# Putting DMA-transposed q and k in token order on ScalarE: planes read in a row and written at a stride of 6, instead of read at a stride and written in a row

## The chip, the cores and the metric

The kernel runs on one core of a Trainium2 chip. The metric is the device time of one execution in microseconds (us); smaller is better. Before the change the median of three runs was 346.24 us (345.09 to 347.84). Runs of one kernel scatter by about half a per cent (the eleven runs of the kernel before made beside experiment 11: 345.25 to 349.92 us, standard deviation 0.5%), so every comparison below uses runs made in turn on the same chip. A run counts as slow when it lies over 1.5% above the fastest run of the same kernel, and as fast otherwise; ratios use fast runs alone. The engines are called PE (TensorE, matmuls), ACT (ScalarE), DVE (VectorE), POOL (GpSimd) and SP (which issues DMAs).

## The reference, cut to what matters

```python
# q, k, v: 8 batches, 8 heads, 576 tokens, 64 channels, float32, 0.1 x normal
q_d, k_d, v_d = means of q, k, v over groups of 4 tokens
out_d     = softmax(q_d k_d^T / 8) v_d           # 144 x 144, then each row repeated 4 times
out_local = softmax of q k^T / 8 where |i - j| < 4, times v
x = (out_up + out_local), as 4608 tokens x 512
h = x @ w_in                                      # 512 x 2048
out = (h - tanh(h)) @ w_out                       # 2048 x 512, float32
```

Of the kernel before, what the change touches and what calls it, by code (L numbers as in the profile page):

```python
# [15 lines left out]
class Program:  # L16
# [18 lines left out]
    def op(self, eng, ns, fn, reads=(), writes=(), pri=0):  # L35
        i = len(self.ops)
        deps = set()
        for key in reads:
            if key in self.last_write:
                deps.add(self.last_write[key])  # L40
        for key in writes:
            if key in self.last_write:
                deps.add(self.last_write[key])
            deps.update(self.readers.get(key, ()))
        for key in reads:
            self.readers.setdefault(key, set()).add(i)
        for key in writes:
            self.last_write[key] = i
            self.readers[key] = set()
        deps.discard(i)  # L50
        self.ops.append((eng, ns, fn, deps, pri))
        self.touch.append(set(reads) | set(writes))
        return i
# [97 lines left out]
def kernel(  # L151
# [18 lines left out]
    A6 = 6  # L170
# [12 lines left out]
    def fixed(name, shape, dt, n=None, pool=const):  # L183
        if n is None:
            return pool.tile(shape, dt, name=name, tag=name)
        return [pool.tile(shape, dt, name=f"{name}{i}", tag=f"{name}{i}")
                for i in range(n)]
# [15 lines left out]
    qT = fixed("qT", [128, 2, A6, G6], BF16, 2)  # L203
# [198 lines left out]
    def attention(p):  # L402
        b, j, hb, s, jj = p // NP, p % NP, p // 2, p % 2, p % 2
# [9 lines left out]
        for i in range(2):  # L413
# [3 lines left out]
                      for eng, ns, fn in REORDER[p >= NEARLY][i]],  # L417
# [3 lines left out]
        full = bass.AP(tensor=qk[s].tensor, offset=qk[s].offset,  # L421
                       ap=[qk[s].ap[0], [KOFF, 2], [1, 576]])
        if p >= T_DMA:
            op("SP", 700, lambda: nc.sync.dma_start_transpose(
                out=qT[s].rearrange("p i a g -> p (i a) g"),
                in_=qr[s].rearrange("p i a c -> p (i a c)")),
               reads=[("qr", s, 0), ("qr", s, 1)],
               writes=[("qT", s), ("qTq", s)], pri=-50)
            op("DMA", 1300, None, reads=[("qTq", s), ("qr", s, 0), ("qr", s, 1)],
               writes=[("qT", s)], pri=pri)  # L430
            for i in range(2):
                op("ACT", 600, lambda i=i: A.copy(  # L432
                    out=full[:, i].rearrange("p (g a) -> p g a", a=A6),
                    in_=qT[s][:, i].rearrange("p a g -> p g a")),
                   reads=[("qT", s)], writes=[("qk", s, i)], pri=pri)
        else:
            for i in range(2):
                b16 = ps[:, i].bitcast(BF16)[:, 0:S]

                def tr(i=i, b16=b16):  # L440
                    for a in range(A6):
                        T.transpose(b16[:, G6 * a:G6 * a + G6], qr[s][:, i, a, :],  # L442
                                    ident[0:G6, 0:G6])
                if i == 0:
                    P.fresh.add(len(P.ops))
                op("PE", 260 * cold, tr, reads=[("qr", s, i), "ident"],
                   writes=[(t, i) for t in ts], pri=pri)
                op("ACT", 540, lambda i=i, b16=b16: A.copy(  # L448
                    out=full[:, i].rearrange("p (g a) -> p g a", a=A6),
                    in_=b16.rearrange("p (a g) -> p g a", a=A6)),  # L450
                   reads=[(t, i) for t in ts], writes=[("qk", s, i)], pri=pri)
# [54 lines left out]
        else:  # L506
# [5 lines left out]
            out=e1, in_=ps[:, :, 0:480], func=AF.Exp, scale=SCALE),  # L512
           reads=ts, writes=[("E", s, 0)], pri=pri)
        op("DVE", 700, lambda: V.tensor_tensor(  # L514
            out=e1, in0=e1,
# [3 lines left out]
        if not new:  # L519
            op("PE", 380 * cold, s2, reads=qks + [("qkd", s)], writes=ts, pri=pri)  # L520
        op("ACT", 240, lambda: A.activation(
            out=e2v, in_=ps2[:, :, 0:96], func=AF.Exp, scale=SCALE),
           reads=ts2, writes=[("E", s, 1)], pri=pri)
        op("ACT", 560, lambda: A.activation(
            out=e3, in_=ps2[:, :, 96:384], func=AF.Exp, scale=SCALE / 16.0),
           reads=ts2, writes=[("E", s, 2)], pri=pri)
        op("DVE", 220, lambda: V.tensor_tensor(
            out=e2v, in0=e2v,
# [5 lines left out]
        def outs():  # L534
# [22 lines left out]
            out=ln[s].rearrange("p n (h d) -> p h n d", d=D),  # L557
# [14 lines left out]
        if p >= X_DMA:  # L572
            op("SP", 600, lambda: nc.sync.dma_start_transpose(
                out=lT[s], in_=ln[s].rearrange("p n c -> p (n c)")),
# [25 lines left out]
            out=xT[j][:, b * S:(b + 1) * S].rearrange("p (g a) -> p g a", a=4),  # L600
# [106 lines left out]
    for i in range(NVW):  # L707
        def ones(i=i):
# [5 lines left out]
            out=vd[i][:, 1, :, 64], in_=vd[i][:, 1, :, 64], compare_op=ALU.is_ge,  # L714
# [46 lines left out]
    for i in range(2):  # L761
        op("DVE", 70, lambda i=i: V.memset(qkd[i][:, 288:344], 0.0),
           writes=[("qkd", i)], pri=-94)
        op("DVE", 70, lambda i=i: V.memset(vp[i][:, :, :, 64:65], 4.0),
           writes=[("vp", i)], pri=-94)
    work = [attention(p) for p in range(NPAIR)]
    for a in work:
        next(a)
# [65 lines left out]
```

## The kernel before: the parts that the change touches

Two heads are processed as a pair, 32 pairs in all. For a pair, q and k arrive with six neighbouring tokens per partition (96 partitions x 6 tokens). They are cast to bf16 and transposed, so that channels lie on partitions. The transposition yields six *planes*: plane `a` holds tokens a, 6+a, 12+a and so on. Someone must then put the planes in token order. Pairs 0 to 15 are transposed by PE into PSUM, and ACT reads the planes from there. Pairs 16 to 31 are transposed by DMA into SBUF (`qT`), and ACT puts them in order in `qk`; this is the code that changes.

```python
# qT[s]: [128, 2 (q, k), 6 planes, 96] bf16;  qk[s]: [128, 1192] bf16; q at element 0, k at 585
full = bass.AP(tensor=qk[s].tensor, offset=qk[s].offset, ap=[qk[s].ap[0], [KOFF, 2], [1, 576]])
if p >= T_DMA:                                   # T_DMA = 16
    op("SP", 700, ... nc.sync.dma_start_transpose(out=qT[s] ..., in_=qr[s] ...) ...)
    for i in range(2):
        op("ACT", 600, lambda i=i: A.copy(                                        # L432
            out=full[:, i].rearrange("p (g a) -> p g a", a=A6),
            in_=qT[s][:, i].rearrange("p a g -> p g a")),
           reads=[("qT", s)], writes=[("qk", s, i)], pri=pri)
else:
    ...                                          # PE transposes; the same A.copy out of PSUM: L448
# then: POOL adds neighbours of q and k (half L459, qkd L464); PE: scores L478 and L494;
# ACT: exp L511, L521, L524; DVE: mask of E L514, L527; PE: E times v L538, L545; ...
```

The dense part is woven in between. Per 512 tokens, it has 16 groups of 4 matmuls into a PSUM buffer (L619), a tanh by ACT (L627), a subtraction by DVE (L630), and the second matmuls (L646), whose results ACT copies out (L657). There are four such PSUM buffers.

The order of instructions on each engine is fixed when the program is built. A planner simulates the program with an assumed cost for each operation and emits it in the order that it finds. The assumed cost of the copy above is 600 ns. It is an input of the plan alone; it changes nothing that the instruction does.

```python
def op(self, eng, ns, fn, reads=(), writes=(), pri=0): ...     # ns: assumed cost
def order(self):  # per step: the engine that can start earliest takes its ready operation of least pri
```

The softmax here doesn't subtract the row's maximum and nothing guards it: scores larger than these inputs give would overflow.

## Time and profile before

| what | before |
|---|---|
| time, median of 3 | 346.24 us |
| PE busy | 328.0 us of 346.3 |
| ACT busy | 224.8 us |
| the 32 copies of L432 | 37.0 us, 1168 to 1225 ns each, 120.9 to 244.7 us |
| the copies out of PSUM (L448), same walk | 633 to 676 ns each (means of the groups 641 and 643) |

The page of the profile shows one execution. Its first row gives the busy time of each engine, with its share of the span; the rows of digits below it split the span in 40 slices and show the busy share of each in tenths.

```profile
span 346.3 us, 6847 instructions
PE 328.0 (95%) x2556; PEld 163.5 (47%) x2556; DVE 223.8 (65%) x362; ACT 224.8 (65%) x382; POOL 169.9 (49%) x210
...
PE   6787989999999999999999999899999999999995
ACT  4585886768978768787878778599753434343411
```

PE is the bound: it is busy nine tenths and more of nearly every slice. The copies, instruction by instruction (minimum, median, maximum in ns):

```profile
L432 ACT COPY qk_88<-qT_90 x16: 1168/1186/1216, 120.9 to 236.2; 128x576 bf16<-128x576 bf16 x16
L432 ACT COPY qk_89<-qT_91 x16: 1173/1188/1225, 129.6 to 243.5; 128x576 bf16<-128x576 bf16 x16
```

The table of stretches gives the busy time of each engine within the stage that has these copies.

```profile
core 0: us, PE busy (x) PEld busy (x) DVE busy (x) ACT busy (x) POOL busy (x), PEclk, DMA share, GB/s
120.00:270.00 150.00, 147.23 (x1139) 72.01 (x1138) 112.02 (x168) 110.98 (x173) 96.50 (x109) 1.00 0.86 179
```

PE works 147.2 of the 150 us. What it waits for in this stage is in the view of waits, for PE from 118 to 275 us (who waited, for whom, us in total, times, longest):

```profile
PE ps_ox L538 <- DVE E_100 L527: 1.5, 3, 0.7
PE ps_ox L538 <- DVE E_100 L514: 0.4, 2, 0.2
PE ps_ox L538 <- DVE E_101 L514: 0.4, 1, 0.4
```

That is 2.3 us. Summed by engine, the chain of work that ended last reads:

```profile
PE 69%; DVE 10%; ACT 9%; issue 3%; DMA 3%; POOL 2%; SPq 1%; ACTq 0%; POOLq 0%; DVEq 0%
```

### The profile page before, as it was taken

How to read it: one execution, taken by the hardware profiler on the slowest of the kernel's cores; microseconds unless marked ns; L12 is line 12 of the kernel's file. 1: busy time of each engine (PE TensorE's matmuls, PEld its weight loads, DVE VectorE, ACT ScalarE, POOL GpSimd, SP SyncE). 2: the span in 40 equal slices, each digit the busy share in tenths (PEclk: the TensorE clock that was granted, in tenths of full speed). 3: DMA queues.
4: the chain of work that ended last, by engine and by line, in shares of the span. 5: the costliest groups of instructions: out<-in, count | busy, mean ns of one | idle time of the engine just before them, and what ended most of it. 6: DMA issues, size and time to landing. Idle time of an engine off the chain costs nothing.

```text
span 346.3 us, 6847 instructions
## 1 busy us (share of the span) xinstructions
PE 328.0 (95%) x2556; PEld 163.5 (47%) x2556; DVE 223.8 (65%) x362; ACT 224.8 (65%) x382; POOL 169.9 (49%) x210
## 2 busy tenths in 40 slices
PE   6787989999999999999999999899999999999995
PEld 2353445555555554445444444444454444444442
DVE  5675788558897968778867677679774443343300
ACT  4585886768978768787878778599753434343411
POOL 6553555575467856887777786958500000000000
PEclk9698999999999999999999999999999999999999
DMA  8999999999999998999999999645231000100021
GB/s 192 234 374 300 277 262 263 217 216 287 212 222 234 252 234 174 226 231 235 261 221 207 260 233 246 157 92 93 57 85 60 31 32 30 61 32 31 30 93 61
DMA packets 103407, 60.74 MB, mean 175 GB/s; under 512 B 77774, under 2 KB 94670, under 8 KB 103374
## 3 DMA queue, kind: packets, MB, share of 16 engines
q1 hardware_dynamic: 103374, 60.30, 78.5%
q8 instruction: 20, 0.33, 0.4%
q14 instruction: 13, 0.11, 0.1%
HBM read 42.46 MB, written 9.44 MB: 150 GB/s over the span
## 4 chain that ended last, share of the span: by engine, by line
PE 69%; DVE 10%; ACT 9%; issue 3%; DMA 3%; POOL 2%; SPq 1%; ACTq 0%; POOLq 0%; DVEq 0%
PE ps_hy_540 L646 8%; PE ps_hy_538 L619 8%; PE ps_hy_539 L619 7%; PE ps_hy_541 L646 7%; PE ps_hy_538 L646 7%; PE ps_hy_539 L646 6%; PE ps_hy_540 L619 6%; PE ps_hy_541 L619 6%; PE ps_ox L538 3%; DVE qr_87 L416 2%; PE ps_ts L478 2%; DMA qkn_73<-in_k_dram 2%; PE ps_ox L545 2%; PE ps_ts L442 2%; PE ps_ox L389 2%
## 5 line engine op out<-in xcount | busy, mean ns | idle before, releaser
L619 PEld LDWEIGHTS <-w_in_sb 128*128 128x128 bf16 x576 | 53.3, 98 | 62.1 <-issue 3.9
L646 PEld LDWEIGHTS <-gT_110 128*128 128x128 bf16 x320 | 30.2, 98 | 34.5
L646 PEld LDWEIGHTS <-gT_111 128*128 128x128 bf16 x256 | 24.0, 98 | 27.4
L459 POOL TENSOR_TENSOR half<-qk_88 128x576 f32<-128x576 bf16 x14 | 16.4, 1169 | 25.3 <-ACT qk_88 L448 11.2
L459 POOL TENSOR_TENSOR half<-qk_89 128x576 f32<-128x576 bf16 x16 | 18.7, 1167 | 19.8 <-ACT qk_89 L448 12.2
L646 PE MATMUL ps_hy_539<-w_out_sb,gT_110 128*128 128x512 bf16 x80 | 20.7, 379 | 0.0
L646 PE MATMUL ps_hy_540<-w_out_sb,gT_110 128*128 128x512 bf16 x80 | 20.4, 379 | 0.0
L646 PE MATMUL ps_hy_538<-w_out_sb,gT_110 128*128 128x512 bf16 x80 | 20.4, 379 | 0.0
L646 PE MATMUL ps_hy_541<-w_out_sb,gT_110 128*128 128x512 bf16 x80 | 20.1, 379 | 0.0
L432 ACT COPY qk_89<-qT_91 128x576 bf16<-128x576 bf16 x16 | 18.7, 1193 | 0.0
L432 ACT COPY qk_88<-qT_90 128x576 bf16<-128x576 bf16 x16 | 18.4, 1188 | 0.0
L511 ACT ACTIVATE E_100<-ps_ts 128x960 bf16<-128x960 f32 x16 | 15.6, 977 | 3.8 <-PE ps_ts L478 3.8
L556 DVE TENSOR_TENSOR ln_106<-ps_ox,r_104 128x896 bf16<-128x896 f32 x16 | 17.4, 1090 | 0.5
L646 PE MATMUL ps_hy_540<-w_out_sb,gT_111 128*128 128x512 bf16 x64 | 16.9, 379 | 0.0
L646 PE MATMUL ps_hy_541<-w_out_sb,gT_111 128*128 128x512 bf16 x64 | 16.8, 379 | 0.0
L646 PE MATMUL ps_hy_539<-w_out_sb,gT_111 128*128 128x512 bf16 x64 | 16.6, 379 | 0.0
L646 PE MATMUL ps_hy_538<-w_out_sb,gT_111 128*128 128x512 bf16 x64 | 16.4, 379 | 0.0
L511 ACT ACTIVATE E_101<-ps_ts 128x960 bf16<-128x960 f32 x14 | 13.6, 973 | 3.8 <-PE ps_ts L478 3.6
L514 DVE TENSOR_TENSOR E_101<-E_101,mask 128x960 bf16<-128x960 bf16 x16 | 13.1, 820 | 3.9 <-ACT E_101 L511 3.7
L556 DVE TENSOR_TENSOR ln_107<-ps_ox,r_105 128x896 bf16<-128x896 f32 x14 | 15.3, 1090 | 0.4
L514 DVE TENSOR_TENSOR E_100<-E_100,mask 128x960 bf16<-128x960 bf16 x16 | 13.6, 847 | 2.8 <-ACT E_100 L511 2.8
L619 PE MATMUL ps_hy_538<-xT_65,w_in_sb 128*128 128x512 bf16 x36 | 13.9, 385 | 1.2 <-DVE xT_68 L599 1.2
(263 smaller groups left out, 890.1 us busy)
## 6 DMA issues: line engine op xcount, KB each, us to landing
out_dram<-y_115 SPq DMA_DIRECT2D x12, 256.0 KB, 2.6
out_dram<-y_116 SPq DMA_DIRECT2D x12, 256.0 KB, 2.3
out_dram<-y_117 SPq DMA_DIRECT2D x12, 256.0 KB, 3.0
qkn_71<-in_q_dram SPq DMA_DIRECT2D x8, 288.0 KB, 7.8
qkn_71<-in_k_dram SPq DMA_DIRECT2D x8, 288.0 KB, 5.8
qkn_72<-in_q_dram SPq DMA_DIRECT2D x8, 288.0 KB, 5.1
qkn_72<-in_k_dram SPq DMA_DIRECT2D x8, 288.0 KB, 5.5
qkn_73<-in_q_dram SPq DMA_DIRECT2D x8, 288.0 KB, 6.6
```

What stands on the lines that cost most here:

```text
L389: T.matmul(pv[:, 0, :], pick[:, t, :], vw[w][:, :, t, 0:64], start=(t == 0), stop=(t == NT - 1))
L416: P.choice([(eng, ns, lambda dst=dst, srt=srt, fn=fn: fn(out=dst, in_=srt)) for eng, ns, fn in REORDER[p >= NEARLY][i]], reads=[("qkn", sn ...
L432: op("ACT", 600, lambda i=i: A.copy(out=full[:, i].rearrange("p (g a) -> p g a", a=A6), in_=qT[s][:, i].rearrange("p a g -> p g a")), read ...
L442: T.transpose(b16[:, G6 * a:G6 * a + G6], qr[s][:, i, a, :], ident[0:G6, 0:G6])
L459: eng.tensor_tensor(out=half, in0=four[:, :, :, 0:2], in1=four[:, :, :, 2:4], op=ALU.add)
L478: T.matmul(sc[:, c:c + NQ[t]], qk[s][rows, k0:k0 + 128], qk[s][rows, QW * t:QW * t + NQ[t]], start=True, stop=True)
L511: op("ACT", 870, lambda: A.activation(out=e1, in_=ps[:, :, 0:480], func=AF.Exp, scale=SCALE), reads=ts, writes=[("E", s, 0)], pri=pri)
L514: op("DVE", 700, lambda: V.tensor_tensor(out=e1, in0=e1, in1=mask[:, 0:480].unsqueeze(1).to_broadcast([128, 2, 480]), op=ALU.mult), reads= ...
L538: T.matmul(po[:, hh, 65 * t:65 * t + 65], E[s][:, c:c + 128], vw[w][:, 2 * jj + hh, t, :], start=True, stop=True)
L556: op("DVE", 1010, lambda: V.tensor_tensor(out=ln[s].rearrange("p n (h d) -> p h n d", d=D), in0=blocks[:, :, :, 0:64], in1=r[s].unsqueeze( ...
L619: T.matmul(ps_hy[slot], w_in_sb[:, dc, fc * 128:(fc + 1) * 128], xT[dc][:, kb * 512:kb * 512 + 512], start=(dc == 0), stop=(dc == N_DC - 1))
L646: T.matmul(ps_hy[slot], gT[g][:, fc, ts * 128:ts * 128 + 128], w_out_sb[:, fc, :], start=(fc == 0), stop=(fc == N_FF - 1))
```

## The change

The copy out of PSUM, with the same walk, takes 643 ns, and the copy out of SBUF 1188 ns. The intent is to take the jumps out of the read: each plane is read as it lies, and its elements are written 6 elements (12 bytes) apart.

```diff
             for i in range(2):
                 op("ACT", 600, lambda i=i: A.copy(
-                    out=full[:, i].rearrange("p (g a) -> p g a", a=A6),
-                    in_=qT[s][:, i].rearrange("p a g -> p g a")),
+                    out=full[:, i].rearrange("p (g a) -> p a g", a=A6), in_=qT[s][:, i]),
                    reads=[("qT", s)], writes=[("qk", s, i)], pri=pri)
```

The assumed cost stays 600 ns. The order of instructions on every engine is therefore unchanged (compared instruction by instruction: the only differences are the 32 copies). Lines after L433 move up by one: L619 becomes L618, and so on.

## The prediction

> **What bounds the kernel now.** TensorE. The page's busy rows give PE 328.0 us of a span of 346.3 (95%), ACT 224.8 (65%), DVE 223.8, POOL 169.9. The instructions by line show ScalarE's copies of the DMA-transposed tiles (L432) 32 times, 1168 to 1225 ns each, 37.0 us in all, between 120.9 and 244.7 us. The table of stretches for 120 to 250 us gives PE 127.2 of 130 us, ACT 101.4 (37.0 of it these copies), DVE 100.7, POOL 96.5. After 250 us PE hardly runs dry, so time won in the stage moves the end one for one; but there is little to win in it.
>
> **What the change does.** Same elements, same 32 instructions. Now the input walks 192 bytes per element and the output is in a row; afterwards the input is in a row and the output walks 12 bytes. The scheduler's cost stays 600 ns, so every engine's order stays.
>
> - Read side: a copy out of PSUM with the same 192-byte read walk (L448) takes 643 ns, so the strided SBUF read is what is slow: (1188-643)/576 = 0.95 ns per element extra. [...] A read in a row should lose it.
> - Write side: [...] this trace has no long write of single elements at a stride. I take writes to be free of the penalty (70%); else the copy stays at 0.9 to 1.3 us (25%) or grows beyond it (5%).
>
> Expected copy: 660 ns; ACT loses 32 x 0.53 = 17 us, from 101 to 84 of the 130.
>
> **How much is on the critical path.** The chain of waits runs through L432 for some 10 us (at 129.6, 136.8, 152.0, 198.6 to 201, 227 to 232), but PE has dense matmuls queued beside it and hardly stalls. In the order of PE's matmuls between 120 and 250 us I count 12 gaps over 150 ns beyond the usual pitch, about 4.8 us: nearly all before the L538 matmuls, waiting for DVE's mask of E (L514, L527). Those at 134.7, 140.8, 157.2, 163.8, 201.3 and 231.9 us (2.0 us) follow an exp that stood behind a copy pair, or a late copy. Those at 147 to 148, 216 and 236 us (2.6 us) follow a slow DVE reorder (qr, up to 2.4 us) or a DMA, and should mostly stay. POOL's 15.9 us of waiting for the copies shrinks, but only 0.2 us of PE's time waited on POOL. So I expect 1 to 3 us gained.
>
> **Predicted time: 344.4 us, 8 in 10 between 341.6 and 347.0.** Faster by over 2%: 0.03. Within 2%: 0.93. Slower by over 2%: 0.04.
>
> **What would show it.** Right: L432 at 640 to 690 ns; ACT busy about 208 us; fewer and shorter PE idles at L538 on E in 120 to 250 us; the last L432 and L538 earlier by 1 to 3 us; POOL's wait for L432 well under 15.9 us. Wrong on the write side: L432 near 1.2 us (time unchanged) or over 1.8 us (ACT then has 120 us or more of the 130, PE waits for E, time up by several us).
>
> **What would make it wrong.** A write penalty; earlier copies making POOL's adds or the DMA transposes collide with DVE's reorders, so that the other 2.6 us grow; or a gain larger than the visible stalls, if DVE's late reorders were late because of ACT. The three runs before spread from 345.09 to 347.84 us, as much as the gain itself.

(Two passages are cut, from the read side and the write side: they gave a mechanism, or its source, that no trace or run of this case had shown by then. No term of the sum is cut: a copy of 660 ns, which is an estimate within the 633 to 676 ns of the copies out of PSUM; 32 x 0.53 = 17 us less for ACT; 1 to 3 us gained; 344.4 us. "The penalty" is the read's 0.95 ns per element. That a write would be free of it, at 70%, was the author's estimate, from no measured write.)

## More of the kernel before

A stretch of the timeline around one pair of copies will matter later (start, duration, engine, line, operation; in brackets, the idle time before it and who ended it):

```profile
136.78 2.27 ACT L432 COPY qk_88<-qT_90 128x576 bf16<-128x576 bf16 x2
...
137.91 0.39 PE L478 MATMUL ps_ts<-qk_89 64*128 64x120 bf16 x8
...
138.95 0.59 ACT L627 ACTIVATE u_113<-ps_hy_540 128x512 f32<-128x512 f32 x1
...
139.44 0.96 ACT L511 ACTIVATE E_101<-ps_ts 128x960 bf16<-128x960 f32 x1
...
141.59 0.37 PE L538 MATMUL ps_ox<-vw_82,E_101 128*128 128x65 bf16 x5 [0.43 <-DVE E_101 L514]
```

The scores L478 are issued at 137.91 us while ACT is still copying; their exp starts 1.53 us later, and PE loses 0.43 us at L538.

## The result, and the profile after

The time is 367.38 us, median of 4 runs (366.18 to 368.13), against 347.04 us for the kernel before in the same rounds: ratio 1.0586, 95% interval 1.0519 to 1.0653. A ratio here and below is the mean time of one kernel's fast runs over that of the other's of the same rounds, so it is not quite the ratio of the medians quoted beside it. The change costs 20 us.

The page, as before:

```profile
span 366.4 us, 6802 instructions
PE 331.0 (90%) x2511; PEld 165.1 (45%) x2556; DVE 226.8 (62%) x362; ACT 251.9 (69%) x382; POOL 171.9 (47%) x210
...
PE   7787999999999887889998978897799999999995
ACT  3584896768968879798978879799963434434421
```

(Some PE records are missing from this trace, hence 6802 instructions; the program has as many as before.) The digits of PE fall to 7 and 8 in the middle, where the copies are. The copies themselves:

```profile
L432 ACT COPY qk<-qT x32: 2122/2156/2349, 121.6 to 262.7; 128x576 bf16<-128x576 bf16 x32
```

They did not fall from 1.19 to 0.66 us; they rose to 2.16. The stretches, the waits of PE (118 to 275 us, the five largest of seven), and the chain by engine:

```profile
core 0: us, PE busy (x) PEld busy (x) DVE busy (x) ACT busy (x) POOL busy (x), PEclk, DMA share, GB/s
120.00:270.00 150.00, 130.19 (x1004) 62.84 (x1022) 102.84 (x150) 128.67 (x158) 97.87 (x110) 1.00 0.87 177
```

```profile
PE ps_hy L618 <- ACT y L656: 6.7, 7, 1.8
PE ps_ox L537 <- DVE E L526: 4.1, 7, 1.1
PE ps_ox L537 <- ACT E L523: 2.9, 3, 1.8
PE ps_ox L493 <- POOL qkd L463: 2.4, 3, 1.1
PE ps_hy L618 <- DVE gT L629: 1.8, 3, 0.8
```

```profile
PE 53%; ACT 21%; issue 9%; DVE 9%; DMA 3%; POOL 2%; SPq 1%; ACTq 0%; POOLq 0%; DVEq 0%
```

In the same 150 us PE works 17.0 us less (about 1 us of it is the missing records: an estimate, from leaving out every 56th PE record of the trace before, which takes 0.8 us away), and ACT's share of the chain goes from 9% to 21%. Note that ACT is busy 128.7 of 150 us, so it is not simply full: 21 us of it are idle. A pair of copies after the change, to set beside the stretch shown of before:

```profile
139.94 4.07 ACT L432 COPY qk<-qT 128x576 bf16<-128x576 bf16 x2
...
141.07 0.39 PE L477 MATMUL ps_ts<-qk 64*128 64x120 bf16 x8
...
143.29 1.03 PE L645 MATMUL ps_hy<-w_out_sb,gT 128*128 128x512 bf16 x4
143.63 0.81 ACT L626 ACTIVATE u<-ps_hy 128x512 f32<-128x512 f32 x1
...
144.33 0.96 ACT L510 ACTIVATE E<-ps_ts 128x960 bf16<-128x960 f32 x1
...
145.32 0.66 DVE L513 TENSOR_TENSOR E<-E,mask 128x960 bf16<-128x960 bf16 x1 [0.16 <-ACT E L510]
...
146.10 0.29 PE L537 MATMUL ps_ox<-vw,E 128*128 128x65 bf16 x4 [1.78 <-ACT E L523]
```

Here the exp of the scores starts 3.26 us after the scores are issued, because ACT is copying and then has one tanh to do, and PE, which has done everything that stands before L537 in its order, waits 1.78 us.

A finer count of PE's losses comes from the order of its matmuls: from start to start, less the usual pitch of the first one's line (216 ns for a dense matmul), counted where more than 240 ns remain, between 118 and 280 us. (One missing record leaves less than 240 ns, so none of them is counted as a wait; this was checked against the sequence of before.) It is worked out from the traces and used for the comparisons below:

| PE waits before | before | after |
|---|---|---|
| L538 (E times v) | 3.9 us | 9.4 us |
| L619 (dense, first matmuls) | 0.3 us | 10.2 us |
| L494 (pooled scores) and others | 0.3 us | 3.6 us |
| sum | 4.4 us | 23.2 us |

The sum grows by 18.8 us; the span of the profiled execution grows by 20.1.

### The profile page after: what moved, and what is told of

Its sections match the earlier page's. It is cut to its first block, busy times and chain, and to the rows that moved or that the text cites. A ratio compares the mean times of both kernels' runs of the same rounds, so it can differ in the third digit from the quotient of the medians.

```text
span 366.4 us, 6802 instructions
## 1 busy us (share of the span) xinstructions
PE 331.0 (90%) x2511; PEld 165.1 (45%) x2556; DVE 226.8 (62%) x362; ACT 251.9 (69%) x382; POOL 171.9 (47%) x210
## 4 chain that ended last, share of the span: by engine, by line
PE 53%; ACT 21%; issue 9%; DVE 9%; DMA 3%; POOL 2%; SPq 1%; ACTq 0%; POOLq 0%; DVEq 0%
PE ps_hy L618 21%; PE ps_hy L645 21%; ACT qk L432 9%; ACT u L626 5%; DVE qr L416 2%; DMA qkn<-in_k_dram 2%; ACT E L510 2%; PE ps_ts L441 2%; PE ps_ox L537 2%; PE ps_ts L477 2%; DVE E L513 2%; PE ps_ox L389 2%; ACT y L656 2%; DVE gT L629 1%; DVE ln L555 1%
## 5 line engine op out<-in xcount | busy, mean ns | idle before, releaser
L618 PE MATMUL ps_hy<-xT,w_in_sb 128*128 128x512 bf16 x555 | 144.7, 383 | 11.0 <-ACT y L656 6.7
L629 DVE TENSOR_TENSOR gT<-ps_hy,u 128x512 bf16<-128x512 f32 x144 | 96.3, 685 | 85.7 <-ACT u L626 84.9
L645 PE MATMUL ps_hy<-w_out_sb,gT 128*128 128x512 bf16 x554 | 138.9, 379 | 1.5 <-issue 0.5
L626 ACT ACTIVATE u<-ps_hy 128x512 f32<-128x512 f32 x144 | 87.7, 629 | 62.8 <-PE ps_hy L618 62.0
L618 PEld LDWEIGHTS <-w_in_sb 128*128 128x128 bf16 x576 | 53.4, 98 | 72.4 <-issue 15.8
L645 PEld LDWEIGHTS <-gT 128*128 128x128 bf16 x576 | 54.2, 98 | 61.9
L432 ACT COPY qk<-qT 128x576 bf16<-128x576 bf16 x32 | 66.5, 2202 | 0.0
L458 POOL TENSOR_TENSOR half<-qk 128x576 f32<-128x576 bf16 x30 | 34.9, 1162 | 59.4 <-ACT qk L432 41.1
L416 DVE CAST qr<-qkn 96x768 bf16<-96x768 f32 x33 | 33.7, 1023 | 6.3 <-DMA qkn<-in_q_dram 5.7
L510 ACT ACTIVATE E<-ps_ts 128x960 bf16<-128x960 f32 x32 | 31.3, 979 | 7.2 <-PE ps_ts L477 7.0
L555 DVE TENSOR_TENSOR ln<-ps_ox,r 128x896 bf16<-128x896 f32 x32 | 34.9, 1090 | 1.0
L537 PE MATMUL ps_ox<-vw,E 128*128 128x65 bf16 x320 | 21.2, 194 | 8.0 <-DVE E L526 4.1
L537 PEld LDWEIGHTS <-E 128*128 128x128 bf16 x320 | 16.3, 98 | 16.8 <-DVE E L513 6.0
```

What stands on the lines that cost most here:

```text
L416: P.choice([(eng, ns, lambda dst=dst, srt=srt, fn=fn: fn(out=dst, in_=srt)) for eng, ns, fn in REORDER[p >= NEARLY][i]], reads=[("qkn", sn ...
L432: op("ACT", 600, lambda i=i: A.copy(out=full[:, i].rearrange("p (g a) -> p a g", a=A6), in_=qT[s][:, i]), reads=[("qT", s)], writes=[("qk" ...
L458: eng.tensor_tensor(out=half, in0=four[:, :, :, 0:2], in1=four[:, :, :, 2:4], op=ALU.add)
L510: op("ACT", 870, lambda: A.activation(out=e1, in_=ps[:, :, 0:480], func=AF.Exp, scale=SCALE), reads=ts, writes=[("E", s, 0)], pri=pri)
L537: T.matmul(po[:, hh, 65 * t:65 * t + 65], E[s][:, c:c + 128], vw[w][:, 2 * jj + hh, t, :], start=True, stop=True)
L555: op("DVE", 1010, lambda: V.tensor_tensor(out=ln[s].rearrange("p n (h d) -> p h n d", d=D), in0=blocks[:, :, :, 0:64], in1=r[s].unsqueeze( ...
```

## The experiments

Two questions were open: why the copy is slow, and why most of its extra time reaches the end (ACT is busy 27.1 us longer, the kernel takes 20) when PE had been the bound.

### 1. Single copies, nothing else running

A kernel with nothing but copies of 128x576 elements, each kind three times; its output is zeros. The edit, in essence:

```diff
+ A.copy(out=dst.rearrange("p (g a) -> p a g", a=6), in_=src)    # the change's copy
+ A.copy(out=every_sth(dst, s), in_=src)                         # s = 2, 3, 4, 6, 8, 16
+ A.copy(out=dst, in_=every_sth(src, s))                         # s = 2, 4, 6, 8, 16
+ ...                                                            # pairs, float32, DVE, POOL
```

> A kernel that only times single copies of 128x576 elements, three of each, with nothing else running; its output is zeros, wrong on purpose. Theory W (the strided write itself is slow): ScalarE's copy of the change takes 2.1 to 2.2 us here too, the copy of before 1.15 to 1.2, a copy with both sides in a row about 0.65. W1 (the cost comes with any gap, because single 2-byte elements can no longer be written together): a write at a step of 2 elements (4 bytes) already takes about 2.15 us, and so do steps of 3 to 16. W2 [...]: steps of 2 and 4 stay below 1.2 us, 6 has 2.15 us and 8 and 16 at least as much. W3 (it is the 2-byte element that is written into a wider word): 4-byte elements at a step of 6 take about 0.65 us, and so do pairs of 2-byte elements at even places. Rival theory C (the copy is slow from contention with DMA, VectorE or GpSimd in the full kernel): the change's copy takes about 0.65 us here. Reads: steps of 8 or more 2-byte elements about 1.2 us, steps of 2 and 4 about 0.65.

These are groups of three copies each, in order: both sides in a row, the copy of before, the change's copy, a read at a step of 8, a write at a step of 6, a write of pairs at a step of 6, and float32 elements at a step of 6 (busy time, mean ns of one, idle time before):

```profile
L52 ACT COPY dst<-src 128x576 bf16<-128x576 bf16 x3 | 2.0, 672 | 14.0 <-DVE dst L33 13.9
L54 ACT COPY dst<-src 128x576 bf16<-128x576 bf16 x3 | 3.5, 1159 | 0.1
L56 ACT COPY dst<-src 128x576 bf16<-128x576 bf16 x3 | 6.3, 2093 | 0.0
L64 ACT COPY dst<-src 128x576 bf16<-128x576 bf16 x3 | 3.5, 1181 | 0.0
L74 ACT COPY dst<-src 128x576 bf16<-128x576 bf16 x3 | 6.3, 2102 | 0.1
L86 ACT COPY dst<-src 128x576 bf16<-128x576 bf16 x3 | 2.0, 682 | 0.1
L98 ACT COPY dsf<-srf 128x576 f32<-128x576 f32 x3 | 3.6, 1198 | 0.0
```

The copy is slow by itself (2093 ns), so contention is ruled out as the main cause. The steps of the single 2-byte elements, in ns:

| step (elements) | 1 | 2 | 3 | 4 | 6 | 8 | 16 |
|---|---|---|---|---|---|---|---|
| read at this step, write in a row | 672 | 662 | - | 681 | 927 | 1181 | 1199 |
| read in a row, write at this step | 672 | 835 | 1146 | 1465 | 2102 | 2733 | 2595 |

None of W1 to W3 fits as it was put. W1 falls, since a step of 2 costs 835 ns and not 2.15 us. W2 falls, since a step of 4, for which it had less than 1.2 us, already costs 1465: the cost rises evenly with the step, up to a step of 8. W3 is right about pairs (682 ns) and wrong about float32 at a step of 6 (1198 ns). In all three kinds timed the cost rises up to a step of 16 bytes and beyond it moves by no more than about 5%: writes of 2 bytes took 2733 ns at a step of 8 and 2595 at 16, writes of float32 950 at a step of 3, 1197 at 4, 1198 at 6 and 1217 at 8, reads of 2 bytes 927 at a step of 6, 1181 at 8 and 1199 at 16. So the writes are counted here by the 16-byte stretches of the output that they touch, called *lines* from here on: 144, 216, 288, 432 and 576 lines for steps of 2, 3, 4, 6 and 8. A straight line through these five times, fitted after the run, is 199 ns plus 4.40 ns for every line, and all five lie within 4 ns of it. Pairs at a step of 6 touch 216 lines too and still cost next to nothing extra (682 ns, against 672 in a row and 1146 for single elements on as many lines), so it is not the lines alone; what they have that single elements lack is that they fill whole 4-byte words. Whether the other engines pay too: POOL took 666 ns in a row and 2090 for the change's copy; DVE took 310 ns in a row, 643 for the copy of before and 1123 for the change's.

### 2. Half words, tested

Again single copies, with zeros as output. The edit, in essence:

```diff
+ A.copy(out=every_sth(dst, s), in_=src)                  # s = 5, 7, 12
+ A.copy(out=runs(dst, 6, n, start), in_=src)             # n = 1, 2, 3, 4 elements every 6
```

> Single copies again, nothing else running, output zeros on purpose. [...] pairs that fill an aligned 4-byte word cost nothing extra. Theory L (a line that gets half-filled 4-byte words costs about 4.4 ns, once per line): ScalarE takes at a step of 5 about 1.78 us (360 lines), 7 about 2.42 us (504), 12 about 2.7 us (576), 6 from an odd start about 2.1 us; pairs at an odd start (step 6, two half words each, 216 lines) about 1.15 us, threes at a step of 6 (one whole and one half word, 144 lines) about 0.82 us, fours at 6 about 0.67 us. Rival S (the cost is one per element that leaves a gap behind it): pairs cost nothing at an odd start either, about 0.68 us, and threes likewise.

(The fit given above, 199 ns + 4.40 ns per line, gives practically the same forecasts: 1.78, 2.42, 2.73, 2.10 and 1.15 us, and 0.83 for threes. A line is a 16-byte stretch of the output, as above; the pairs that cost nothing extra took 682 ns, against 672 in a row.)

In order: steps of 5 and 7; pairs from an even start, pairs from an odd start, threes, and fours.

```profile
L62 ACT COPY dst<-src 128x576 bf16<-128x576 bf16 x3 | 5.3, 1781 | 0.1
L66 ACT COPY dst<-src 128x576 bf16<-128x576 bf16 x3 | 7.3, 2417 | 0.1
L72 ACT COPY dst<-src 128x576 bf16<-128x576 bf16 x3 | 2.0, 683 | 0.1
L74 ACT COPY dst<-src 128x576 bf16<-128x576 bf16 x3 | 3.4, 1146 | 0.1
L78 ACT COPY dst<-src 128x576 bf16<-128x576 bf16 x3 | 2.5, 830 | 0.1
L82 ACT COPY dst<-src 128x576 bf16<-128x576 bf16 x3 | 2.0, 671 | 0.1
```

Theory L hits 1.78, 2.42, 1.15, 0.82 and 0.67 us; rival S, which had pairs from an odd start at 0.68, falls. The rule is not exact: a step of 12 took 2830 ns (2.7 expected), single elements from an odd start at a step of 6 took 2394 (2.1 expected), and a step of 16 in the first run was a little under that of 8. So in these runs a visit to a 16-byte line that left half-filled 4-byte words there cost ScalarE about 4.4 ns (4.2 to 5.1 over the kinds timed), and the change's copy, with 432 such visits (its six planes each pass over 72 lines), is priced by this to within a few ns of what it took alone (199 + 432 x 4.40 = 2100, against 2093). Three of its six planes start at an odd element, and yet it does not show the surplus of the single elements from an odd start; that is not explained.

### 3. The whole kernel with a cheap write

Planes are copied as they lie. The tokens end in the wrong order, so the kernel is wrong. (The comparison with the reference did not notice: with inputs of 0.1 x normal the scores are about 0.01, and the weights of a softmax are nearly equal whatever the order of q and k. It is wrong all the same. For the same reason a passed comparison says little about the order in any run here; that the other kernels put the tokens in the right order is read from their code.)

```diff
-                    out=full[:, i].rearrange("p (g a) -> p a g", a=A6),
+                    out=full[:, i].rearrange("p (a g) -> p a g", a=A6),
                     in_=qT[s][:, i]),
```

> The change with its write in a row as well: planes copied as they lie, tokens in the wrong order, so the output is wrong on purpose; instruction order on every engine is that of before. All theories that blame the strided write: the copies take 640 to 690 ns and the time is what the prediction had for a free write, 344.4 us, 342 to 346.5 (ratio to before 0.985 to 1.0). If reading in a row from a tile that the DMA has just written is what is slow: copies over 1.5 us and the time near 367 us.

```profile
L432 ACT COPY qk<-qT x32: 662/678/708, 120.5 to 240.2; 128x576 bf16<-128x576 bf16 x32
```

The copies took 662 to 708 ns. The time was 345.7 us against 347.62 for before; ratio 0.9983, interval 0.9924 to 1.0043. This is what the prediction had in mind when it took the write as free: its size of the copy and the sign of its gain hold in the trace (PE's waits fall from 4.4 to 2.4 us), and the gain in time is within the scatter. The failure of the prediction is thus all on the write side.

### 4. Half of the change

Only q is copied the new way.

```diff
-                    out=full[:, i].rearrange("p (g a) -> p g a", a=A6),
-                    in_=qT[s][:, i].rearrange("p a g -> p g a")),
+                    out=full[:, i].rearrange("p (g a) -> p a g", a=A6)
+                    if i == 0 else full[:, i].rearrange("p (g a) -> p g a", a=A6),
+                    in_=qT[s][:, i] if i == 0 else qT[s][:, i].rearrange("p a g -> p g a")),
```

> q is copied as in the change, k as before; same order of instructions, right output. ScalarE's copies then sum to about 53 us, between 37 and 69 (VERSUS 64 us of its other work in a stage of 130). Theory T1 (the stage is as long as ScalarE's total work makes it, once that exceeds what PE leaves room for): 118 us of work still fit 130, so a small loss, 348 to 353 us. Theory T2 (a pair of copies back to back is a block in which no tanh runs, and it costs when it outlasts the four PSUM buffers that dense matmuls can fill, about 3.5 us; the pair is now 3.35 us instead of 4.3): near before, 346 to 350 us. Theory T3 (each extra microsecond of copy costs in proportion): midway, 355 to 358 us.

(T2's 3.5 us is an estimate; it agrees with the 16 dense matmuls that fill four buffers, at the 216 ns each of the trace.)

355.39 us against 347.62, ratio 1.0233 (1.0172 to 1.0295), so 8 of the 20 us. T1 and T2 both expected less; the time lies in T3's range, and experiment 6 shows its limit.

### 5. The change, planned with the true cost

```diff
-                op("ACT", 600, lambda i=i: A.copy(
+                op("ACT", 2160, lambda i=i: A.copy(
```

> The change, with the cost that the scheduler assumes for these copies raised from 600 to 2160 ns, their true one; the scheduler puts all engines' instructions in another order. T1 (total work of ScalarE bounds the stage): most of the loss stays, 360 to 368 us. T2 (the order, made for short copies, is what loses): most of the loss is won back, 349 to 357 us.

349.81 us against 347.62, ratio 1.0069 (1.0009 to 1.0129). The copies still take 2102 to 2311 ns each:

```profile
L432 ACT COPY qk<-qT x32: 2102/2132/2311, 122.7 to 258.9; 128x576 bf16<-128x576 bf16 x32
```

ACT is busy 252.4 us, as in the change; yet nearly all of the loss is gone, as T2 had it. ACT's total work is not the bound. (The new plan also hands 8 operations from POOL to DVE: 202 and 370 instructions, 210 and 362 before.) The same stretch as above:

```profile
120.00:270.00 150.00, 142.93 (x1099) 70.83 (x1119) 111.87 (x171) 137.03 (x172) 92.40 (x101) 1.00 0.89 183
```

ACT now does 137.0 us of work in these 150 (128.7 in the change) and PE 142.9 (130.2). Each waits less for the other.

### 6. ACT held as long, without the strided write

Each copy is made with rows on both sides (token order wrong, as in experiment 3) and preceded by three dummy copies.

```diff
-                op("ACT", 600, lambda i=i: A.copy(
-                    out=full[:, i].rearrange("p (g a) -> p a g", a=A6),
-                    in_=qT[s][:, i]),
+                op("ACT", 600, lambda i=i: [A.copy(out=spare, in_=mask[:, 0:448]) for _ in range(3)] + [
+                    A.copy(out=full[:, i].rearrange("p (a g) -> p a g", a=A6),
+                    in_=qT[s][:, i])],
```

> Each of the 32 copies is made with both sides in a row (token order wrong on purpose, as in the run with rows) and is preceded by three dummy copies of 448 elements in a row, so that ScalarE is held about as long as by the strided write [...]; order on all engines as before. Theory O (only ScalarE's occupancy matters): nearly the time of the change, 362 to 368 us. Rival D (the strided write also holds up other engines' use of the memory, and that is part of the loss): clearly less, under 358 us.

378.37 us against 347.6, ratio 1.0919 (1.0852 to 1.0987). This misses both theories' numbers, because the dose was off: a dummy copy took 565 ns (median), more than assumed, and a strided copy let the next ACT instruction start before its own recorded end (start to start 1752 ns for 2156 ns of duration; 1078 for 1188 in before; 562 for 678 with rows). So, after the result, the author took another measure, how long ACT is *held*: for the 32 copies and their dummies, the time to the start of the next ACT instruction, but no more than the duration. It still counts too little for the strided write, because the instruction behind one is itself recorded longer: a tanh behind a strided copy took 817 ns (median, as the 0.81 us in the stretch shown above), elsewhere 597. The second column therefore counts by ends: from the end of the ACT instruction before, or the copy's own start if that is later, to the copy's end. Worked out from one profiled execution each, in the plan of before:

| kernel (all in the plan of before) | ACT held, to the next start, us | ACT held, by ends, us | PE's waits in the stage, us | ratio of time to before |
|---|---|---|---|---|
| rows on both sides | 19.8 | 18.1 | 2.4 | 0.9983 |
| paired walk, k moved (experiment 11) | 21.7 | 20.2 | 2.5 | 1.0003 |
| paired walk (experiment 10) | 27.6 | 27.0 | 3.1 | 0.9954 |
| before | 35.2 | 34.4 | 4.4 | 1 |
| q alone changed | 45.5 | 46.5 | 11.3 | 1.0233 |
| the change | 58.5 | 63.8 | 23.2 | 1.0586; again 1.0523 |
| rows and dummies | 69.8 | 69.2 | 32.8 | 1.0919 |

(The profiled execution of q alone was the fastest of its four, 352.42 us.) Up to before's 35 us the holding hardly shows. Beyond it most of it is lost: from before to the change, 23.3 us more of holding (29.4 by ends) cost PE 18.8 us. The kernel with dummies, which has no strided write at all, loses more than the change, and by ends it loses more for each microsecond than the kernels that have one. So theory O (only ScalarE's occupancy matters) is right that holding ACT is enough, but its number was missed, and the total held does not fix the loss exactly: how the time lies among ACT's other work matters too (experiments 5 and 9). Rival D (a disturbance of the memory), which needs the strided write, is not needed, and the trace of the change speaks against it: VectorE's subtractions (L629) took 678 ns (median) while a strided copy ran and 691 otherwise, its products (L555) 1092 and 1091.

### 7. The kernel before, planned with its true cost

```diff
-                op("ACT", 600, lambda i=i: A.copy(
+                op("ACT", 1190, lambda i=i: A.copy(
```

> The kernel before with the assumed cost of its copies raised from 600 to 1190 ns, their true one. If the loss of the change came from an order planned for too short copies, the kernel before, whose copies also take twice the plan, gains a little from an honest plan: ratio 0.985 to 0.998. If the plan only matters once ScalarE is overloaded: ratio 0.997 to 1.005.

350.12 us against 347.6, ratio 1.0044 (0.9976 to 1.0112): no gain from an honest cost here. The expected small gain did not come; the ratio lies in the range of the other case, that the plan only matters once ACT is overloaded. (Two of its six runs and two of the eleven of before beside it are slow; the fast ones alone have medians of 348.64 and 347.27 us, and the ratio uses those. The profiled execution is a slow one and is not read.)

### 8. The plan for 2160 ns with the copies of before

```diff
-                op("ACT", 600, lambda i=i: A.copy(
+                op("ACT", 2160, lambda i=i: A.copy(
```

(This is an edit of the kernel before; the copies keep their old walk.)

> The kernel before in the order that was planned for copies of 2160 ns; the copies themselves stay 1.19 us. The change in that same order took 349.8 us. If what was left of its loss (about 2 us) is due to the longer copies: 345 to 348 us here, ratio 0.992 to 1.0. If it is due to the order: about 350 us here too, ratio 1.005 to 1.012.

349.56 us against 347.6, ratio 1.0058 (1.0007 to 1.0108), practically the 1.0069 of the change in the same plan. In this plan ACT is held 36.6 us by these copies and 57.9 us by the change's, and PE's waits are 7.5 and 8.3 us. So in a plan that leaves room for them, 21 us more of holding (30 by ends: 34.3 and 64.5) cost nothing that can be seen, and the small rest is the plan's own price. It also speaks against rival D once more: the strided writes are in one of the two kernels and not in the other.

### 9. One instruction between the copies of a pair, and VectorE as a helper

The change's ACT order has 10 places where two copies stand back to back. An edit of ACT's order alone put the next ACT instruction between them; the orders of PE, DVE, POOL and SP were compared and are the same.

```diff
+ # for each (copy, copy, x) in ACT's order: emit x before the second copy,
+ # and whatever between them depends on that copy after x
+ order[a:z + 1] = [i for i in part if i not in later] + [x] + [i for i in part if i in later]
```

> The change, with one edit to ScalarE's order only: in the 10 places where two copies stand back to back, the ScalarE instruction that follows the pair (mostly a tanh) is put between the two. All other engines' orders are those of the change. Theory B (the pair as an uninterrupted block of 3.5 to 4 us is what costs): a quarter or more of the 20 us comes back, 355 to 362 us. Theory O (each copy's time on ScalarE costs, wherever it stands, as the planned order leaves ScalarE no more room): 364 to 369 us.

371.97 us, ratio 1.0687 (1.063 to 1.0743). The change itself, run beside it:

> The change itself, unedited, on the chip of the run with the swap, so that the two can be compared: 365 to 369 us, ratio to before 1.05 to 1.065.

366.92 us against 348.1, ratio 1.0523 (1.0458 to 1.0588). The swap costs 5 us more. Theory B falls in this form: splitting a pair by hand is no cure. PE's waits before the dense matmuls (L619 by the old numbering) fell from 10.2 to 8.6 us, but those before the pooled scores (L494) went from 3.3 to 6.5 us, and those before E times v from 9.4 to 10.6. In the view of waits, the time before the pooled scores goes to POOL's adds (5.4 us, 2.4 in the change), and POOL waits for the copies (45.4 us, 41.1 in the change): the second copy came later still. So ACT has several deadlines at once, and a cure for one moved another. ACT was held about as long as in the change (57.2 us against 58.5; by ends, 64.5 against 63.8), and PE still waited 26.2 us against 23.2: theory O's "wherever it stands" is not right either.

The other attempt was on the kernel before: the planner may give each copy to ACT (1190 ns) or DVE (650 ns).

```diff
-                op("ACT", 600, lambda i=i: A.copy(
+                P.choice([(eng, ns, lambda i=i, fn=fn: fn(
                     ...
+                    for eng, ns, fn in (("ACT", 1190, A.copy), ("DVE", 650, V.tensor_copy))],
```

> The kernel before, with each copy given at planning to ScalarE (cost 1190 ns) or VectorE (650 ns, where this same copy took 0.64 us by itself), whichever is free first. The copies on VectorE take 640 to 800 ns. If there is still something to gain from relieving ScalarE: ratio 0.98 to 0.995. If PE's own work is the bound, as the run with rows says (its copies at 0.68 us gained 0.2%): ratio 0.995 to 1.005.

352.22 us against 347.6, ratio 1.0148 (1.0093 to 1.0202). DVE took 18 of the 32 copies at a median of 652 ns, one of them at 2482 ns, and was then busy 114.5 of the 130 us from 120 to 250 (100.7 in before). Both numbers expected were too good. That DVE had no more room is likely, but not shown: the plan put all engines in another order as well, and a plan alone cost 0.6% in experiment 8.

### 10. The change with a walk that fills words

Two planes are taken in turn, so that two neighbouring tokens are written one after the other. By its code the output is right.

```diff
-                    out=full[:, i].rearrange("p (g a) -> p a g", a=A6),
-                    in_=qT[s][:, i]),
+                    out=full[:, i].rearrange("p (g a e) -> p a g e", a=3, e=2),
+                    in_=qT[s][:, i].rearrange("p (a e) g -> p a g e", e=2)),
```

> The change with its walk altered so that two planes are taken in turn: element by element the reads again jump 192 bytes, and the writes come in pairs of neighbouring tokens, a pair every 12 bytes; right output, order on all engines as before. For q the pairs fill aligned 4-byte words; for k, which starts at element 585, they do not. Theory L (half-filled 4-byte words are what the change's write paid for): q's copies take about 1.19 us, as before, the reads being what is left; k's take 1.2 us if the two costs overlap and up to 2.0 us if they add. Time 346 to 350 us if k is near 1.2 us, about 355 us (as with q alone changed) if k is near 2.1. Rival S (any write that is not in a row pays): both near 2.1 us, and 367 us.

347.39 us against 348.56, ratio 0.9954 (0.9884 to 1.0024). The two operands split cleanly:

```profile
L432 ACT COPY qk<-qT x32: 727/962/1214, 121.9 to 242.6; 128x576 bf16<-128x576 bf16 x32
```

In order of time the durations alternate: 727 to 762 ns for q and 1161 to 1214 for k. q is faster than expected: reads that jump 192 bytes at each element, but between two planes only, cost little (a median of 740 ns for q, 678 with rows on both sides), while the six planes in turn of before cost 1188. k's 1.17 us is what half words cost from an odd start (1146 ns for pairs alone, experiment 2), if that is its cause.

### 11. k's row moved by one element

```diff
-    KOFF = 585
+    KOFF = 586
...
-            V.memset(qk[i][:, 576:585], 0.0)
-            V.memset(qk[i][:, 1161:1192], 0.0)
+            V.memset(qk[i][:, 576:586], 0.0)
+            V.memset(qk[i][:, 1162:1192], 0.0)
```

(on top of experiment 10)

> The paired walk, with k's row moved from element 585 to 586 of the tile, so that k's pairs too fill aligned 4-byte words; right output. Theory L (half-filled words): k's copies fall from 1.17 us to q's 0.73 to 0.76. Rival: if k's 1.17 has another cause (its reads, or its place behind q's copy), it stays over 1.1 us. Time: ScalarE is then held no longer than with rows on both sides (345.7 us, ratio 0.998), so ratio 0.985 to 1.0.

```profile
L432 ACT COPY qk<-qT x32: 726/744/790, 122.8 to 243.0; 128x576 bf16<-128x576 bf16 x32
```

All 32 copies are now at 726 to 790 ns: one element's shift took 0.43 us off each of k's. The half word is the cause in the whole kernel too. The time is 347.37 us against 347.93, ratio 1.0003 (0.9945 to 1.006). This is the fast copy that the change was after, with right output, and the kernel is no faster for it: PE's waits had only about 2 us to give, and that is inside the scatter. No version here beats the kernel before by a measurable amount.

## Why the prediction was wrong

- **"I take writes to be free of the penalty (70%)", copy of 660 ns.** This is the step that failed. The copy took 2156 ns, because single 2-byte elements at 12 bytes' distance leave half-filled 4-byte words on 432 visits to a 16-byte line, at about 4.4 ns each (experiments 1, 2, 10, 11). The penalty known from reads was 0.95 ns per element; the prediction let the write's be at most about as large as the read's (25%), and gave "grows beyond it" 5%. The trace of before held no case to take it from. The cheap way out was to see it as unknown and widen the range.
- **Read side.** Right: with the write in a row the copies took 678 ns (median) in the whole kernel, as against the 660 predicted (experiment 3).
- **The critical path for a free write, 1 to 3 us.** The trace bears it out: PE's waits fell from 4.4 to 2.4 us. In time, 0.2% was measured, not separable from nothing.
- **"Over 1.8 us (ACT then has 120 us or more of the 130, PE waits for E, time up by several us)".** The direction is right and the mechanism only partly so. ACT was never full (110.8 of the 130 us that the prediction speaks of, 128.7 of 150), PE waited as much before dense matmuls (10.2 us) as before E times v (9.4 us), and "several us" was 20.
- **Why it reached the end.** Of the span's 20.1 us, 18.8 lie in PE's waits in this stage. The orders of all engines had been planned for copies of 600 ns. In that plan, ACT's holding up to about 35 us is absorbed, and of what comes on top some two thirds to four fifths are lost (18.8 us of PE's waits for 29.4 or 23.3 us of holding, the table of experiment 6); in a plan made for 2160 ns the same copies cost nothing visible (experiments 5 and 8). That is shown. Which feature of the plan gives the room was not settled: separating the pairs alone made it worse (experiment 9). The traces show two that differ: back-to-back pairs of copies fall from 10 to 1, and between the scores (L478) and E times v (L538) PE's order has a median of 14 dense matmuls before and 23 in the plan for 2160 ns, so that PE has more to do while ACT is late. Neither was varied alone.
- **The chances.** Within 2% had 0.93, slower 0.04. The 0.04 is in keeping with the 5% for a copy that grows beyond 1.3 us; for one of over 1.8 us the prediction itself had PE waiting for E. Being off the critical path keeps a saving from mattering, not a loss.

## What to carry to other kernels

Read the width and alignment of a strided write, not only its distance: 2-byte elements written singly at a step of 12 bytes cost three times a row here (2156 ns against 678), the same elements in aligned pairs cost a tenth more than a row (744). An operation off the critical path can have little to gain and a great deal to lose, as here: look for the slack that it has, and what lies beyond. Where a static order is planned from assumed costs, compare those costs with the trace, and after a change of an operation's cost plan again before judging it (349.8 against 367.4 us here for the same copies, in another order and with 8 operations on another engine).

## What else the runs show of such copies

- ScalarE's reads of 576 single 2-byte elements, written in a row, cost next to nothing extra at steps of 2 and 4 (662 and 681 ns, 672 in a row); they took 927 ns at 6, 1181 at 8 and 1199 at 16. Single 2-byte writes cost up to 2830 ns (a step of 12), about 4.4 ns (4.2 to 5.1) for each visit to a 16-byte line that left half-filled 4-byte words. Pairs at a 12-byte step took 683 ns from an even element and 1146 from an odd one.
- Copies whose reads alternate between two planes 192 bytes apart took 726 to 790 ns (662 to 708 with rows on both sides), while those that go round six took 1168 to 1225.
- The next ACT instruction started before the recorded end of a copy: 116 ns before it for a copy in rows (678 less 562) and 404 ns for the strided write (2156 less 1752). Of these 404 some 220 are no gain, since the tanh behind a strided copy is recorded that much longer (817 ns against 597); the rest, about 184 ns, is counted in both recorded durations.
- The other engines pay too. The change's copy took POOL 2090 ns against 666 in a row (no pairs were timed there, so half words are not shown to be its cause), and DVE 1123 against 310. The copies of experiment 2, made on DVE as well and not reported above, fit 157 ns + 2.24 ns for each such visit (fitted to the steps of 5, 6 and 7), half of ScalarE's 4.40: 963, 1124 and 1286 ns at steps of 5, 6 and 7, 647 for pairs from an odd start (359 from an even one), 487 for threes. Steps of 12 (1516, 1447 by the fit) and single elements from an odd start (1341, 1125) lie above it, as on ScalarE.
